# A sketched-attention and gated-convolution kernel: bf16 matmuls in 64-column tiles, one store per output block, and a new order of steps

## The chip, the cores and the metric

The kernel runs on one core of a Trainium2 chip. The metric is the device time of one execution in microseconds (us). The *span*, from the first to the last event of the core, is some 1.7 us shorter. All times within a trace are counted from the start of the span.

A run is called slow when it is more than 1.5% above the fastest of its kernel.

## The reference, cut to what matters

```python
def phi(x):                                   # S1, S2: 8 x 32
    a = einsum('rd,bhsd->bhsr', S1, x);  b = einsum('rd,bhsd->bhsr', S2, x)
    return einsum('bhsi,bhsj->bhsij', a, b).reshape(..., 64)
q_p, k_p = phi(q), phi(k)                     # q, k, v: (4, 4, 1088, 32) float32
kv  = einsum('bhsf,bhsd->bhfd', k_p, v);   z = sum(k_p, axis=2)
x   = einsum('bhsf,bhfd->bhsd', q_p, kv) / (einsum('bhsf,bhf->bhs', q_p, z)[..., None] + 1e-06)
x   = x.transpose(0, 2, 1, 3).reshape(4, 1088, 128)
gate_pre = causal convolution of x along s with conv_w (5 taps, per channel)
out = (sigmoid(gate_pre) * (x @ w_val)) @ w_out          # (4, 1088, 128)
```

## The kernel before: the parts that matter here

The names that the profile shows, in the order of the data: `kT`, `qT` are transposes of k and q in 32x32 blocks on VectorE; `abk`, `abq` their projections on TensorE (f32, 64-column tiles); `ab_sb` the copy of `abk`, `phik` the products a*b of it; `kv` the sums over the sequence (f32, 32-column tiles); `phiq` the normalised features of q (bf16); `pt` their transposes on TensorE and `phiT` the copies of those. For each batch `wg` (kv with the convolution's taps) and `kw` (kv with w_val) are the weights of the gate `g_ps` and the value `v_ps`. `gate` is the sigmoid, `gv` the product, `o_ps` the output, `o_sb` its copy that is stored. There are twelve pieces of k and of q (four batches by three) and 13 output groups. The first 128-column matmuls, `warm_ps`, work on zeros to keep TensorE busy.

The order of all steps is one list, and the program gives every engine its instructions in that order. In the words of that list, `kab.5` is the `abk` of piece 5, `wm.0.512` a zero matmul of 512 columns.

```python
    SP.dma_start(out=s_raw[:r], in_=S1)
    SCA.dma_start(out=s_raw[r:], in_=S2)
    load_units(k, k_sb, 0, 0, 1)              # on SyncE (SP)
    load_units(k, k_sb, 0, 1, U)
...
                PE.transpose(                 # q_pt: full 128-column tiles
                    pt[:, g, t], phq[i, x][:, 2 * t + g].rearrange("p h i j -> p (h i j)"), identity
                )
...
            PE.matmul(                        # g_val
                v_ps[:, :n], lhsT=kw[b][:, g, :], rhs=flat[:, g, c0 : c0 + n],
                start=(g == 0), stop=(g == 1),
            )
...
            if one_store(i):                  # g_st: the last four groups
                (SCA if i == len(GROUPS) - 1 else SP).dma_start(out=rows, in_=src)
            else:                             # the first nine: four stores, or six
                for m in range(nm):
                    SP.dma_start(out=rows[:, m], in_=src[J * m : J * (m + 1)])
...
    ORDER = """
    s2 wm.0.512 wm.1.512 f3.3 f3.1 pad f1 kT.0 f3.0 mz kab.0 kcp.0 cw wm.2.512 kz.0 wm.3.256 kT.1
    ...
```

The whole kernel:

## Time and profile before

| | before |
|---|---|
| median of three runs (lowest, highest), us | 63.55 (62.36, 63.57) |
| span of the profiled run, us | 59.9 |
| first `abk`, first `abq` start | 5.19, 9.74 |
| first `g_ps` starts, last `gv` ends | 18.35, 54.54 |
| last computing ends, last SyncE issue ends | 55.28, 57.08 |

The table cuts the run into three parts: a *start* to the first `abq`, a *middle* to the end of the last `gv` (44.8 us), and a *tail* to the end of the span (5.3 us).

### The profile page before, as it was taken

How to read it: one execution, taken by the hardware profiler on the slowest of the kernel's cores; microseconds unless marked ns; L12 is line 12 of the kernel's file. 1: busy time of each engine (PE TensorE's matmuls, PEld its weight loads, DVE VectorE, ACT ScalarE, POOL GpSimd, SP SyncE). 2: the span in 40 equal slices, each digit the busy share in tenths (PEclk: the TensorE clock that was granted, in tenths of full speed). 3: DMA queues.
4: the chain of work that ended last, by engine and by line, in shares of the span. 5: the costliest groups of instructions: out<-in, count | busy, mean ns of one | idle time of the engine just before them, and what ended most of it. 6: DMA issues, size and time to landing. Idle time of an engine off the chain costs nothing.

```text
span 59.9 us, 2553 instructions
## 1 busy us (share of the span) xinstructions
PE 50.7 (85%) x1003; PEld 36.2 (60%) x1003; DVE 44.3 (74%) x127; ACT 34.7 (58%) x96; POOL 31.8 (53%) x81
## 2 busy tenths in 40 slices
PE   1998988999799899987999999779999999994000
PEld 0224556887586697866985868458876676661000
DVE  2289949998699997994998899357794999836000
ACT  0830241638976688999328759315988776945000
POOL 5653589899995386998829959800420040000000
PEclk9999999999999999999999999999999999999985
DMA  0299997998894587720767421324042223421380
GB/s 0 53 341 370 375 280 236 285 241 238 252 341 141 171 236 211 250 69 5 236 188 189 144 66 44 104 70 109 3 111 69 55 77 99 107 67 34 73 305 5
DMA packets 9254, 9.35 MB, mean 156 GB/s; under 512 B 1941, under 2 KB 9242, under 8 KB 9242
## 3 DMA queue, kind: packets, MB, share of 16 engines
q1 hardware_dynamic: 9072, 9.05, 50.7%
q8 instruction: 8, 0.13, 0.9%
q10 hardware_dynamic: 170, 0.13, 0.7%
q14 instruction: 4, 0.03, 0.3%
HBM read 6.95 MB, written 2.23 MB: 153 GB/s over the span
## 4 chain that ended last, share of the span: by engine, by line
PE 60%; DVE 15%; ACT 8%; issue 4%; POOL 4%; DVEq 0%; ACTq 0%
PE kv L72 12%; PE g_ps L72 11%; PE abq L72 10%; PE abk L72 7%; PE v_ps L72 5%; PE pt L72 5%; PE warm_ps L72 4%; DVE gv L72 4%; DVE wg L72 3%; POOL phik L72 3%; PE wg_ps L72 2%; PE o_ps L72 2%; DVE o_sb L72 2%; ACT wg L72 2%; DVE kT L72 1%
## 5 line engine op out<-in xcount | busy, mean ns | idle before, releaser
L72 POOL TENSOR_TENSOR phik<-ab_sb 128x256 f32<-128x256 f32 x33 | 19.9, 629 | 0.3 <-ACT ab_sb L72 0.3
L72 DVE TENSOR_TENSOR phiq<-an,abq 128x768 bf16<-128x768 f32 (+2 forms) x13 | 11.2, 881 | 0.1
L72 PE MATMUL g_ps<-phiT,wg 128*64 128x384 bf16 (+3 forms) x130 | 11.0, 307 | 0.1
L72 ACT COPY phiT<-pt 128x768 bf16<-128x768 bf16 (+2 forms) x13 | 9.7, 753 | 1.9 <-PE pt L72 1.7
L72 PEld LDWEIGHTS <-wg 128*64 128x64 bf16 x130 | 7.2, 109 | 2.0 <-issue 0.4
L72 ACT ACTIVATE gate<-g_ps 128x384 bf16<-128x384 f32 (+3 forms) x13 | 5.8, 457 | 4.3 <-PE g_ps L72 4.1
L72 DVE TENSOR_TENSOR gv<-gate,v_ps 128x256 bf16<-128x256 bf16 (+3 forms) x14 | 6.1, 456 | 2.8 <-PE v_ps L72 1.5
L72 PE MATMUL abq<-rhsq,qT 128*64 128x96 f32 x144 | 7.7, 251 | 0.2 <-ACT rhsq L72 0.2
L72 PE MATMUL kv<-phik,v_sb 128*32 128x64 f32 x288 | 6.7, 223 | 1.1 <-DVE zm L72 0.6
L72 DVE STREAM_TRANSPOSE kT<-k_sb 128x384 f32<-128x384 f32 x12 | 7.3, 627 | 0.0
L72 PE MATMUL abk<-S,kT 128*64 128x64 f32 x144 | 6.8, 234 | 0.2 <-DVE kT L72 0.2
L72 DVE STREAM_TRANSPOSE qT<-q_sb 128x384 f32<-128x384 f32 x12 | 6.6, 555 | 0.3 <-DMA q_sb<-in_q_dram 0.3
L72 PEld LDWEIGHTS abq<-rhsq,qT 128*64 128x64 f32 x144 | 6.3, 136 | 0.8 <-POOL phiT L72 0.3
L72 PEld LDWEIGHTS abk<-S,kT 128*64 128x64 f32 x144 | 5.6, 144 | 1.7 <-DVE kT L72 1.1
L72 POOL TENSOR_TENSOR prod<-ac 128x96 f32<-128x96 f32 x6 | 2.3, 389 | 7.8 <-ACT ac L72 4.8
L72 PE MATMUL pt<-identity,phiq 128*128 128x128 bf16 x72 | 6.2, 219 | 0.2 <-ACT phiT L72 0.2
L72 ACT COPY ab_sb<-abk 128x192 f32<-128x192 f32 x11 | 3.5, 319 | 4.8 <-PE abk L72 4.7
L72 PE MATMUL warm_ps<-zeros 128*128 128x512 bf16 (+1 forms) x11 | 5.0, 529 | 1.3 <-DVE hm L72 1.3
L72 PEld LDWEIGHTS kv<-phik,v_sb 128*32 128x32 f32 x288 | 4.8, 109 | 2.1 <-DVE zm L72 0.9
L72 PE MATMUL v_ps<-phiT,kw 128*128 128x384 bf16 (+3 forms) x26 | 5.8, 308 | 0.2 <-issue 0.2
L72 PEld LDWEIGHTS <-phiq 128*128 128x128 bf16 x72 | 4.8, 98 | 1.3 <-DVE rden L72 0.4
L72 ACT COPY o_sb<-o_ps 128x384 f32<-128x384 f32 (+3 forms) x13 | 4.8, 399 | 0.9 <-PE o_ps L72 0.8
(77 smaller groups left out, 65.9 us busy)
## 6 DMA issues: line engine op xcount, KB each, us to landing
v_sb<-in_v_dram SPq DMA_DIRECT2D x15, 144.0 KB, 3.7
q_sb<-in_q_dram SPq DMA_DIRECT2D x8, 192.0 KB, 3.5
k_sb<-in_k_dram SPq DMA_DIRECT2D x7, 192.0 KB, 4.2
out_dram<-o_sb SPq DMA_DIRECT2D x24, 48.0 KB, 1.6
q_sb<-in_q_dram SPq DMA_DIRECT2D x4, 160.0 KB, 3.5
k_sb<-in_k_dram SPq DMA_DIRECT2D x3, 160.0 KB, 4.6
k_sb<-in_k_dram SPq DMA_DIRECT2D x1, 384.0 KB, 3.3
out_dram<-o_sb SPq DMA_DIRECT2D x12, 32.0 KB, 1.6
```

The costliest lines, as they stand in the source:

```text
L72: return lambda *a, **k: tc.keep_in_program_order(call(*a, **k))
```

## The change

It has four parts, meant to take work and waits from TensorE, VectorE and SyncE's queue: all bf16 matmuls go in 64-column tiles, so that TensorE changes its tiling mode less often (34 times in the program where it was 53); each output block is stored at once, with its columns in (j,m) order, a row order that makes the store one regular transfer; the first piece of k is issued by ScalarE and the second half of S by SyncE; and the list of steps is a new one. The diff, cut to its core:

```diff
-    SCA.dma_start(out=s_raw[r:], in_=S2)
-    load_units(k, k_sb, 0, 0, 1)
-    load_units(k, k_sb, 0, 1, U)
+    load_units(SCA, k, k_sb, 0, 0, 1)
+    SP.dma_start(out=s_raw[r:], in_=S2)
+    load_units(SP, k, k_sb, 0, 1, U)
...  (the memsets of wg go ahead of the wait for S; the two S products become one;
...   kT of batch 0 is written straight; v of batch 0 is loaded in quarters as the others)
-                PE.transpose(
-                    pt[:, g, t], phq[i, x][:, 2 * t + g].rearrange("p h i j -> p (h i j)"), identity
-                )
+                for y in range(2):
+                    PE.transpose(
+                        pt[R2 * y : R2 * (y + 1), g, t],
+                        phq[i, x][:, 2 * t + g, y].rearrange("p i j -> p (i j)"), identity,
+                    )
...  (v_ps, kw_ps and o_ps are halved in the same way)
+    def by_rows(i, x):
+        lo = 0
+        for _, nc_, nm in blocks(i):
+            hi = lo + nc_ * nm * J
+            yield lo, hi, x[:, lo:hi].rearrange("p (m c j) -> p c j m", m=nm, c=nc_)
+            lo = hi
...  (sigmoid and gv read PSUM through by_rows and write in (j,m) order)
-            if one_store(i):
-                (SCA if i == len(GROUPS) - 1 else SP).dma_start(out=rows, in_=src)
-            else:
-                for m in range(nm):
-                    SP.dma_start(out=rows[:, m], in_=src[J * m : J * (m + 1)])
+            (SCA if i == len(GROUPS) - 1 else SP).dma_start(out=dst, in_=src)
...
-    s2 wm.0.512 wm.1.512 f3.3 f3.1 pad f1 kT.0 f3.0 mz kab.0 kcp.0 cw wm.2.512 kz.0 wm.3.256 kT.1
+    kT.0 s2 wm.0.256 pad kab.0 kcp.0 cw wm.1.512 kT.1 kT.2 kz.0 kab.1 mz kcp.1 kab.2 wm.2.256 kz.1
...  (the whole list differs)
```

More of the change, by code (lines that the diff above doesn't have):

```diff
@@ L106, in load, with load_units @@
         )
-    def load_units(src, dst, b, u0, u1):
+    def load_units(eng, src, dst, b, u0, u1):
         lo, n = NCK * u0 * D, NCK * (u1 - u0) * D
-        SP.dma_start(
+        eng.dma_start(
             out=dst[b].rearrange("p (m x) -> p m x", m=M4)[:, :, lo : lo + n],
@@ L114, in load_units @@
                 tensor=src.tensor, offset=src[b].offset + lo, ap=[[NT * D, P], [TM * D, M4], [1, n]]
-            ),
-        )
-    def v_head(b, h):
-        SP.dma_start(
-            out=v_sb[b][:, h].rearrange("p T d -> p (T d)"),
-            in_=bass.AP(
-                tensor=v.tensor, offset=v[b, h].offset, ap=[[NT * D, J], [TM * D, M4], [1, TM * D]]
             ),
@@ L139, in load_v @@
         for x in (0, 2, 1, 3):
-            (v_head if b == 0 else v_quarter)(b, x)
+            v_quarter(b, x)
     def load_k(b):
@@ L193, with fill_3 @@
         DVE.memset(hm[h * D : (h + 1) * D, h : h + 1], 1.0)
+    wg = [ctile([P, 2, KT, 2 * D], BF16, f"wg{b}") for b in range(B)]
+    def fill_3(eng, b):
+        for x in range(2):
+            eng.memset(wg[b][R2 * x : R2 * (x + 1), :, :, D * (1 - x) : D * (2 - x)], 0.0)
+    fill_3(DVE, 0)
+    fill_3(DVE, 1)
     m2 = ctile([P, 2], F32, "m2")
@@ L204 @@
     keep_warm(2)
-    for x in range(2):
-        DVE.tensor_mul(
-            S3[:, x].rearrange("p (h r) -> p h r", h=H),
-            st_ps[:, x].unsqueeze(1).to_broadcast([P, H, r]),
-            hm.unsqueeze(2).to_broadcast([P, H, r]),
-        )
+    DVE.tensor_mul(
+        S3.rearrange("p x (h r) -> p x h r", h=H),
+        st_ps.unsqueeze(2).to_broadcast([P, 2, H, r]),
+        hm.unsqueeze(1).unsqueeze(3).to_broadcast([P, 2, H, r]),
+    )
     mz4 = ctile([P, H, H], F32, "mz4")
@@ L224 @@
     dcw = ctile([P, KT, D], F32, "dcw")
-    wg = [ctile([P, 2, KT, 2 * D], BF16, f"wg{b}") for b in range(B)]
     POOL.memset(w_val_sb, 0.0)
@@ L263, in fill_2 @@
             POOL.memset(phiT[b][:, :, 0].rearrange("p g (T j) -> p g T j", j=J)[:, :, :, 0:1], 0.0)
-    def fill_3(eng, b):
-        for x in range(2):
-            eng.memset(wg[b][R2 * x : R2 * (x + 1), :, :, D * (1 - x) : D * (2 - x)], 0.0)
     def pad_k():
@@ L305, in k_T @@
         DVE.transpose(
-            out=kT[b][:, u * W : (u + 1) * W].rearrange(
-                "p (t m j) -> p t m j" if b else "p (t j m) -> p t m j", t=NCK, m=M4
-            ),
+            out=kT[b][:, u * W : (u + 1) * W].rearrange("p (t m j) -> p t m j", t=NCK, m=M4),
             in_=k_sb[b].rearrange("p (m u t d) -> p u t m d", m=M4, u=U, t=NCK)[:, u],
@@ L429, in kw_mm @@
         kwp[b] = ps_k.tile([P, 2, P], F32, tag="k", name="kw_ps")
-        PE.matmul(kwp[b], lhsT=kvt[b].rearrange("p x f -> p (x f)"), rhs=w_val_sb, start=True, stop=True)
+        for x in range(2):
+            PE.matmul(
+                kwp[b][R2 * x : R2 * (x + 1)], lhsT=kvt[b][:, x], rhs=w_val_sb, start=True, stop=True
+            )
     def kw_ev(eng, b):
@@ L502, in q_pt @@
             for g in range(2):
-                PE.transpose(
-                    pt[:, g, t], phq[i, x][:, 2 * t + g].rearrange("p h i j -> p (h i j)"), identity
-                )
+                for y in range(2):
+                    PE.transpose(
+                        pt[R2 * y : R2 * (y + 1), g, t],
+                        phq[i, x][:, 2 * t + g, y].rearrange("p i j -> p (i j)"), identity,
+                    )
         pts[i, x] = pt
@@ L524 @@
     GROUPS = [(b, T0, min(TU, NT - T0)) for b in range(B - 1) for T0 in range(0, NT, TU)]
-    ONE = 9
     GROUPS += [(B - 1, 0, 12), (B - 1, 28, 6), (B - 1, 12, 8), (B - 1, 20, 8)]
@@ L553, in g_val @@
         for g in range(2):
-            PE.matmul(
-                v_ps[:, :n], lhsT=kw[b][:, g, :], rhs=flat[:, g, c0 : c0 + n],
-                start=(g == 0), stop=(g == 1),
-            )
-        vps[i] = v_ps
-    def g_sig(i):
-        _, n, _ = columns(i)
-        gate = work.tile([P, W], BF16, tag="gate", name="gate")
-        SCA.activation(out=gate[:, :n], in_=gps[i][:, :n], func=ACT.Sigmoid)
-        gts[i] = gate
+            for y in range(2):
+                ys = slice(P // 2 * y, P // 2 * (y + 1))
+                PE.matmul(
+                    v_ps[ys, :n], lhsT=kw[b][:, g, ys], rhs=flat[:, g, c0 : c0 + n],
+                    start=(g == 0), stop=(g == 1), skip_group_check=True,
+                )
+        vps[i] = v_ps
     def blocks(i):
@@ L570, in blocks, with rows, g_sig @@
         return [(T0, *whole[n])] if n in whole else [(T0, 2, M4), (T0 + 2 * M4, 1, n - 2 * M4)]
-    def one_store(i):
-        return i >= ONE
+    def by_rows(i, x):
[4 more added lines that the diff above has]
+            lo = hi
+    def rows(x, lo, hi, like):
+        return x[:, lo:hi].rearrange("p (c j m) -> p c j m", j=J, m=like.shape[3])
+    def g_sig(i):
+        gate = work.tile([P, W], BF16, tag="gate", name="gate")
+        for lo, hi, x in by_rows(i, gps[i]):
+            SCA.activation(out=rows(gate, lo, hi, x), in_=x, func=ACT.Sigmoid)
+        gts[i] = gate
     def g_gv(eng, i):
@@ L582, in g_gv @@
         gv = work.tile([P, W], BF16, tag="gv", name="gv")
-        lo = 0
-        for _, nc_, nm in blocks(i):
-            hi = lo + nc_ * nm * J
-            order = "p c j m" if one_store(i) else "p c m j"
-            def cols(x):
-                return x[:, lo:hi].rearrange(f"p (m c j) -> {order}", m=nm, c=nc_)
-            eng.tensor_mul(
-                gv[:, lo:hi].rearrange(f"p ({order[2:]}) -> {order}", c=nc_, m=nm), cols(gts[i]), cols(val)
-            )
-            lo = hi
+        for lo, hi, x in by_rows(i, val):
+            eng.tensor_mul(rows(gv, lo, hi, x), rows(gts[i], lo, hi, x), x)
         gvs[i] = gv
@@ L603, in g_out @@
             for c in range(nc_):
-                PE.matmul(
-                    o_ps[: nm * J, c0 + c, :], lhsT=gvs[i][:, lo : lo + nm * J], rhs=w_out_sb,
-                    start=True, stop=True,
-                )
+                for y in range(0, nm * J, P // 2):
+                    PE.matmul(
+                        o_ps[y : y + P // 2, c0 + c, :], lhsT=gvs[i][:, lo + y : lo + y + P // 2],
+                        rhs=w_out_sb, start=True, stop=True,
+                    )
                 lo += nm * J
@@ L625, in g_st @@
             src = osb[i][: J * nm, c0 : c0 + nc_].rearrange("p c e -> p (c e)")
-            rows = o_d[:, T0 : T0 + nm * nc_].rearrange("j (m c) e -> j m (c e)", m=nm)
-            if one_store(i):
-                (SCA if i == len(GROUPS) - 1 else SP).dma_start(out=rows, in_=src)
-            else:
-                for m in range(nm):
-                    SP.dma_start(out=rows[:, m], in_=src[J * m : J * (m + 1)])
+            dst = o_d[:, T0 : T0 + nm * nc_].rearrange("j (m c) e -> j m (c e)", m=nm)
+            (SCA if i == len(GROUPS) - 1 else SP).dma_start(out=dst, in_=src)
             c0 += nc_
@@ L648 @@
     ORDER = """
-    s2 wm.0.512 wm.1.512 f3.3 f3.1 pad f1 kT.0 f3.0 mz kab.0 kcp.0 cw wm.2.512 kz.0 wm.3.256 kT.1
-    sr.0 kT.2 kab.1 kab.2 kp.0.0 kcp.1 srA.1 kz.1 kcp.2 kz.2 wm.4.256 qT.1 qT.0 zm.0 c.0 wm.5.256
-    kpV.2.2 kpV.0.2 qab.0 qab.1 kT.3 kT.5 qcp.0 kp.1.1 kp.1.2 kab.3 f2 qcp.1 kkv.1.2 kpV.2.1 kT.4
-    kp.2.0 kp.1.0 qpr.0 kp.0.1 kkv.2.0 kcp.3 kkv.2.2 kab.5 kkv.1.0 qden.0 qprV.1 qrc.0 kp.3.1 ldq.3
-    kkv.1.1 kkv.2.1 qden.1 kkv.0.2 kkv.0.0 ldk.2 kcp.5 qanV.0 w kp.5.0 qrc.1 qphi.0 kkv.0.1 kvx.0
@@ L654 @@
-    kab.4 qpt.0 kp.3.0 qT.2 qanV.1 kp.5.1 qphi.1 qab.2 kcp.4 qev.0 qcp.2 kp.4.0 qT.3 kvtA.0 ldq.4
-    kp.3.2 qprV.2 kz.3 wgm.0 kz.4 kkv.5.0 kkv.3.1 kz.5 kkv.4.0 ldq.5 zm.1 wge.0.0 wge.0.1 kkv.5.1
-    kkv.3.0 qden.2 c.1 kwm.0 kwe.0 kT.6 qrc.2 qpt.1 kp.4.1 qev.1 qab.3 halo.0 ldk.3 qcp.3 kab.6
-    kp.5.2 kp.4.2 gmm.0 qpr.3 val.0 kcp.6 sig.0 qanV.2 qphi.2 qT.5 qden.3 qpt.2 ldq.8 ldq.6 qrc.3
-    kT.7 qan.3 qphi.3 kkv.3.2 qT.4 kkv.4.1 kkv.4.2 kT.8 kkv.5.2 gvP.0 kvx.1 qev.2 kp.6.2 ldv.2 kab.7
-    qab.5 qcp.5 kcpV.7 qab.4 kT.9 qpr.5 o.0 qpt.3 qcp.4 srA.2 oev.0 wgm.1 gmm.1 kvtA.1 wge.1.0 gmm.2
@@ L660 @@
-    qprV.4 wge.1.1 qden.4 qden.5 qev.3 qrc.4 kp.7.2 qan.4 qrc.5 kab.8 kz.6 ldq.7 f3.2 kcp.8 qanV.5
-    qphi.4 kp.7.0 kp.7.1 kp.6.0 sig.1 haloA.1 kp.8.1 qpt.4 qT.6 val.2 kwm.1 val.1 kz.7 kp.8.0 st.0
-    qphi.5 kkv.8.1 qT.8 kkv.6.2 kz.8 kkv.8.0 kkv.6.0 kkv.7.2 qev.4 kp.8.2 kwe.1 kkv.7.0 gvP.1 sig.2
-    zm.2 ldq.11 kT.10 cV.2 qT.7 kab.9 ldq.9 kcp.9 qab.6 qab.7 gv.2 qcpV.6 kp.6.1 qprV.6 qden.6 gmm.3
-    kab.10 qrc.6 kkv.6.1 srA.3 ldq.10 sig.3 kcp.10 kkv.7.1 kkv.8.2 kvx.2 qpt.5 val.3 wgm.2 qcpV.7
@@ L665 @@
-    kT.11 o.2 qan.6 qphi.6 qev.5 kp.9.1 oev.2 qpr.7 qden.7 wgeV.2.0 gv.3 qab.8 kp.10.2 qcpV.8 qprV.8
-    wge.2.1 kab.11 kp.10.0 qden.8 gmm.4 kcp.11 sig.4 kp.10.1 gmm.5 kp.9.0 ldv.3 sig.5 kz.9 qrc.7
-    qan.7 qrc.8 qan.8 o.3 kp.9.2 val.4 o.1 st.2 qpt.6 qT.10 oev.3 kz.10 kp.11.0 kp.11.2 qphi.7
-    kkv.10.1 kkv.9.0 oev.1 kz.11 qev.6 kkv.9.2 qphi.8 kp.11.1 kkv.11.2 st.3 kkv.10.2 kkv.10.0
-    kkv.11.0 zm.3 kkv.9.1 c.3 gv.4 qT.9 kkv.11.1 val.5 kvtP.2 qpt.7 qab.10 qab.9 o.4 gv.5 qev.7
-    qcp.9 kvxV.3 kwm.2 qcpV.10 qpr.10 haloV.2 qpt.8 oev.4 o.5 qprV.9 qev.8 oev.5 kwe.2 qden.10
@@ L671 @@
-    qden.9 qrc.10 qT.11 gmm.6 gmm.8 sig.6 sig.8 gmm.7 qan.10 qrc.9 wgm.3 sig.7 kvtA.3 val.7 val.6
-    qphi.10 qan.9 qphi.9 qpt.9 wge.3.1 gv.7 qev.9 o.7 qab.11 val.8 st.1 qcp.11 wgeV.3.0 oevV.7 gv.6
-    st.4 qpr.11 qpt.10 halo.3 kwm.3 qev.10 o.6 gv.8 qden.11 o.8 st.5 gmm.10 oevV.6 qrc.11 qanV.11
-    gmm.9 st.7 qphi.11.0 kwe.3 oev.8 sig.10 sig.9 st.6 val.10 qpt.11.0 val.9 qev.11.0 qphi.11.1
-    gv.10 qpt.11.1 qev.11.1 st.8 gv.9 o.10 gmm.11 val.11 oev.10 gmm.12 sig.11 val.12 gv.11 st.10 o.9
-    sig.12 gv.12 o.11 oev.9 st.9 o.12 oev.12 oevV.11 st.11 st.12
+    kT.0 s2 wm.0.256 pad kab.0 kcp.0 cw wm.1.512 kT.1 kT.2 kz.0 kab.1 mz kcp.1 kab.2 wm.2.256 kz.1
@@ new lines @@
+    kcp.2 srA.0 qT.0 kp.0.2 qT.1 kz.2 wm.3.256 sr.1 zm.0 kpV.2.1 kpV.0.0 c.0 wm.4.256 kpV.1.2 kT.3
+    qab.1 ldq.3 qab.0 kp.0.1 kp.1.1 kp.1.0 qcp.1 kT.5 kab.3 qcp.0 kT.4 kcp.3 kp.2.2 f1 qpr.0 kab.5
+    qden.0 kcp.5 qprV.1 kp.2.0 kab.4 qrc.0 kkv.0.2 kp.3.1 kkv.2.0 kcp.4 kkv.1.2 kkv.1.0 kp.3.2
+    qden.1 qanV.0 qrc.1 qphi.0 qan.1 kkv.2.2 kkv.1.1 kkv.2.1 kkv.0.1 kkv.0.0 qT.2 kvxV.0 qpt.0
+    kvtA.0 qev.0 qab.2 kp.5.1 kz.3 wgm.0 kz.4 wge.0.0 kkv.5.1 f2 qphi.1 w kz.5 qcpV.2 kkv.3.1 kp.3.0
+    kp.4.0 halo.0 qprV.2 qden.2 zm.1 kkv.3.2 qpt.1 qT.3 wge.0.1 c.1 kp.5.0 qrc.2 kkv.4.0 qanV.2
@@ new lines @@
+    kkv.3.0 ldk.2 kwm.0 kp.5.2 qphi.2 qev.1 kT.6 kp.4.1 qab.3 ldq.4 kwe.0 gmm.0 qT.4 val.0 qcp.3
+    kab.6 qpr.3 kp.4.2 ldq.5 qpt.2 kkv.4.2 ldk.3 qden.3 qrc.3 qan.3 sig.0 kT.7 kkv.5.2 gvP.0 kcp.6
+    qT.5 ldq.6 kkv.4.1 kkv.5.0 ldv.2 kab.7 qev.2 qphi.3 kp.6.2 qab.4 ldq.7 o.0 kvx.1 kcp.7 kT.8
+    qcpV.4 kT.9 kp.7.1 kp.6.0 qprV.4 wgm.1 oev.0 kp.7.2 kz.6 kvtP.1 qden.4 qrc.4 qT.6 srA.2 wge.1.0
+    st.0 kp.6.1 qanV.4 qT.7 val.2 qab.5 wge.1.1 kab.8 gmm.2 kp.7.0 kcp.8 kwm.1 qpt.3 qcp.5 sig.2
+    qphi.4 gmm.1 gv.2 kz.7 kkv.6.0 kkv.7.2 kp.8.1 qev.3 qpr.5 qden.5 kp.8.2 qrc.5 kwe.1 kz.8 kp.8.0
@@ new lines @@
+    zm.2 qanV.5 sig.1 val.1 srV.3 kab.9 gvP.1 qphi.5 o.2 kT.10 qpt.4 oev.2 kkv.8.0 f3P.2 halo.1
+    ldq.8 ldq.9 qT.8 ldv.3 kkv.6.1 kcp.9 kkv.7.0 f3P.3 kkv.7.1 c.2 kkv.8.1 kkv.8.2 kkv.6.2 o.1 qev.4
+    ldq.10 st.2 kT.11 qab.6 kab.10 gmm.3 qcp.6 qprV.6 qden.6 qrc.6 qanV.6 oev.1 kvx.2 kcp.10 qphi.6
+    val.3 qab.8 qpt.5 sig.3 kp.9.2 gv.3 qcp.8 kz.9 wgm.2 ldq.11 wgeV.2.0 qab.7 kp.9.1 qev.5 kp.10.1
+    qcp.7 o.3 gmm.4 oev.3 wge.2.1 qT.11 sig.4 qT.10 kab.11 gmm.5 qpt.6 qpr.8 kp.9.0 kcp.11 qden.8
@@ new lines @@
+    kp.10.0 val.4 qpr.7 sig.5 kp.10.2 qden.7 qrc.7 qrc.8 qanV.7 kkv.10.2 kvtA.2 kp.11.1 kz.10
+    kkv.10.0 kp.11.0 qphi.7 kkv.9.0 kkv.9.1 kz.11 qan.8 kkv.9.2 kkv.11.1 kkv.10.1 gvP.4 kpV.11.2
+    kkv.11.0 qev.6 st.1 zm.3 kkv.11.2 c.3 qT.9 qphi.8 val.5 halo.2 st.3 qpt.7 o.4 qev.7 qab.9 qab.10
+    qcp.9 oevV.4 gv.5 qpt.8 qcp.10 qpr.9 kvxV.3 o.5 kwm.2 qev.8 oev.5 qpr.10 gmm.6 qden.9 gmm.8
+    kwe.2 qden.10 sig.6 gmm.7 wgm.3 qrc.9 qrc.10 sig.8 qanV.10 sig.7 qan.9 kvtP.3 val.7 qphi.9
+    qphi.10 val.6 wge.3.1 wge.3.0 st.4 qpt.9 val.8 gv.7 o.7 qev.9 gv.6 qab.11 o.6 gv.8 oevV.7 oevV.6
@@ L677 @@
+    qcp.11 qpr.11 qden.11 qpt.10 qrc.11 o.8 qanV.11 qev.10 kwm.3 oev.8 gmm.10 halo.3 gmm.9 kwe.3
+    sig.10 qphi.11.0 st.5 sig.9 val.10 qphi.11.1 qpt.11.0 st.7 val.9 gv.10 qev.11.0 st.6 o.10 oev.10
+    qpt.11.1 st.8 gv.9 qevV.11.1 gmm.11 sig.11 st.10 val.11 gv.11 gmm.12 sig.12 val.12 o.11 o.9
+    oev.11 gv.12 o.12 oev.12 st.11 oevV.9 st.9 st.12
     """
```

## The prediction

*Drain* is the name for the surplus of some 95 ns between the starts of matmuls at a change of tiling mode. The traces show the surplus (150 ns where 56 to 60 were due), not what TensorE does in it.

> **What bounds the kernel now.** I read the page first: busy shares and the chain of work that ended last.
>
> ```profile
> PE 50.7 (85%) x1003; PEld 36.2 (60%) x1003; DVE 44.3 (74%) x127; ACT 34.7 (58%) x96; POOL 31.8 (53%) x81
> ...
> PE 60%; DVE 15%; ACT 8%; issue 4%; POOL 4%; DVEq 0%; ACTq 0%
> ```
>
> TensorE has 60% of the chain, in many small pieces (kv, g_ps, abq, abk, v_ps, pt). VectorE is second, at 74% busy. So what matters most is what TensorE pays per stage, then the two ends of the run, where other things bind. I next read TensorE's timeline where it changes from one kind of matmul to another. Columns: start, length, engine, line, operation, tile form, count.
>
> ```profile
> 13.01 0.57 PE L72 MATMUL abk<-S,kT 128*64 128x64 f32 x12
> 13.51 0.51 PE L72 MATMUL pt<-identity,phiq 128*128 128x128 bf16 x6
> 13.95 0.79 PE L72 MATMUL abq<-rhsq,qT 128*64 128x96 f32 x12
> ...
> 18.35 1.00 PE L72 MATMUL g_ps<-phiT,wg 128*64 128x384 bf16 x10
> 19.29 0.34 PE L72 MATMUL v_ps<-phiT,kw 128*128 128x384 bf16 x1
> ```
>
> One transpose lasts 0.22 us in its record, so the six start every (0.51-0.22)/5, about 56 ns, and the last starts at 13.80. The first abq starts at 13.95, 150 ns later. The surplus is about 95 ns. Backwards likewise: the last abk starts at 13.01+0.57-0.22 = 13.36, the first transpose 150 ns later, where two of abk's matmuls stand some 60 ns apart. From g_ps to v_ps it is about 260 ns where 384 columns take 160. **Each change between a 64-column and a 128-column tile costs about 95 ns**, whatever the types. This kernel has its f32 work and the gate in 64-column tiles, but the bf16 transposes, v_ps, kw and o_ps in full ones.
>
> Then the beginning, on VectorE:
>
> ```profile
> 2.35 0.21 DVE L72 COPY s_nat<-s_raw 16x128 f32<-16x128 f32 x1 [0.70 <-DMA s_raw<-in_S_dram]
> 3.00 0.29 DVE L72 TENSOR_TENSOR S<-st_ps,hm 128x32 f32<-128x32 f32 x2 [0.44 <-PE st_ps L72]
> 3.27 0.98 DVE L72 MEMSET wg<- 64x160 uint32 x4
> 4.28 0.85 DVE L72 STREAM_TRANSPOSE kT<-k_sb 128x384 f32<-128x384 f32 x1
> ...
> 10.86 0.55 DVE L72 STREAM_TRANSPOSE kT<-k_sb 128x384 f32<-128x384 f32 x1
> ```
>
> Four memsets stand before the first k transpose, on the chain, while VectorE had idled 0.70 us before. The first transposes write in (j,m) order and take 0.85 us; later ones write straight and take 0.55.
>
> Then the end: the queue of SyncE, ScalarE's store and the last copies.
>
> ```profile
> 49.98 7.10 SPq L72 DMA_DIRECT2D out_dram<-o_sb  x12
> ...
> 55.32 0.62 ACTq L72 DMA_DIRECT2D out_dram<-o_sb  x1
> ...
> 53.94 0.59 DVE L72 TENSOR_TENSOR gv<-gate,v_ps 128x256 bf16<-128x256 bf16 x1 [0.40 <-ACT gate L72]
> 54.45 0.41 DVE L72 COPY o_sb<-o_ps 128x256 f32<-128x256 f32 x1
> ```
>
> The last block that SyncE stores is ready at 54.86, but SyncE issues its last store only at 57.08, after a backlog of quarter stores. Nothing computes after 55.28; the span ends at 59.9.
>
> [...] The trace has 98 ns for a full bf16 load and 109 for a 64-column one, but they lie beside matmuls; whether they show in the spacing I judge below. [...] for strided PSUM reads no clean case exists in it. [...] a SyncE issue takes 0.4 to 0.6 us.
>
> **The change, part by part.**
>
> *Tile mode.* I counted mode changes in the order of the matmuls of both programs: 53 before, 34 after, so 19 fewer; all but one lie after the start, where the 128-column tiles disappear altogether. 19 x 95 ns = 1.8 us of TensorE. What the halves cost: a transpose becomes two of 64 columns in two tiles that run side by side. g_ps does this already: ten matmuls of 384 columns in 1.00 us, that is five pairs of about 160 ns, the time of one. abk pairs, of 64 columns with two f32 weight loads, stand about 60 ns apart, so a load pair fits in 60. I take 56 to 64 ns per transpose pair, against 56 now: 72 x 0 to 8 ns, at most 0.6 us lost. v_ps, o_ps and kw stream as long as before. Net on TensorE 1.2 to 1.8 us; with TensorE on the chain over most of 9.7 to 46 us, but handing over to VectorE and GpSimd at 22-26, 33-38 and 46-49 us, I count two thirds: **-1.1 us**.
>
> *Start.* The memsets move into VectorE's wait: 1.0 us off. The first k transposes fall from 0.85 to 0.55: three times 0.3. The first k piece leaves ScalarE at 0.81 instead of SyncE at 1.27. Against it, the second half of S goes out second on SyncE, about 0.3 us later, and so does everything from s_nat on. The first transpose should start near 3.5 instead of 4.28 and abk near 4.3 instead of 5.19. The first abq (9.74 now) then comes some 1 to 1.5 us earlier. Not all can survive, since v of the first batch lands only near 9.5 to 10 us: **-0.9 us**.
>
> *Stores.* Four SyncE issues of about 0.42 us become one of about 0.58. The backlog goes. Now it takes 57.08-54.53 = 2.55 us from the end of the last gv to the end of the last issue. After: matmuls 0.3, eviction 0.37, ScalarE's issue 0.62, with gaps 1.4 us; SyncE's last store (eviction 0.56, issue 0.6) fits beside it. **-1.1 us.**
>
> *Order of (j,m) rows.* The late gv, which already reorders, takes 0.81 us for 384 columns and 0.59 for 256:
>
> ```profile
> L72 DVE TENSOR_TENSOR gv<-gate,v_ps x4: 206/460/553, 29.3 to 38.7; 128x384 bf16<-128x384 bf16 x2, 128x256 bf16<-128x256 bf16 x1, 128x64 bf16<-128x64 bf16 x1
> ...
> L72 DVE TENSOR_TENSOR gv<-gate,v_ps x1: 808/808/808, 51.5 to 51.5; 128x384 bf16<-128x384 bf16 x1
> ```
>
> It reads both the gate (SBUF) and v_ps (PSUM) with a stride. After, only PSUM is read with a stride, by the sigmoid and by gv. If SBUF was the cost, every gv takes 0.55 and the tail gains 0.2; if PSUM is as dear, seven earlier gv lose 0.2 each on VectorE and thirteen sigmoids some 0.2 on ScalarE. I hold the first likelier (60%). The sigmoid of the 320-column groups is split, three times 0.15 us on ScalarE, which has room.
>
> *New order.* Going down both VectorE lists with the durations above, VectorE loses some 2 us (fewer and cheaper kT, memsets, copies of ac and wg), GpSimd gains about 2. That unloads the second bound and loads one with 47% idle: **-0.3 us**, uncertain in sign.
>
> Sum: -1.1-0.9-1.1-0.3 = -3.4 us; I take off 0.2 for the strided reads: -3.2 of 59.9, a span of about 56.7. 63.55 x 56.7/59.9 = **60.2 us**.
>
> **Rivals.** (1) *TensorE isn't the bound in the middle*: the 19 drains vanish into waits on VectorE and GpSimd. For it: VectorE is nearly always busy from 9 to 38 us, and phik on GpSimd alone takes 19.9 us. Against: TensorE's 60% of the chain. Then only the two ends count: -1.8 us, about 61.6. (2) *64-column weights are slower*: [...] say 80 ns a pair: 72 x 24 ns = 1.7 us, which eats the drains saved. Against: abk's pairs at 60. About 61.4. (3) *PSUM stride dear and GpSimd late*: phik and gv on GpSimd push kv back; with the first two gains kept about 61.5. (4) *All add up, and the earlier start pulls everything with it*: -4.5 us, about 58.8.
>
> **Range and chances.** Runs of before lie between 62.36 and 63.57, so 1.2 us of spread is there without any change. From rivals 1 to 4: 58.2 to 62.0. Under 2% is 1.3 us; the two ends alone give more, so faster 0.87, same 0.11, slower 0.02.
>
> **What would show it.** Right: pt, v_ps and o_ps in 64-column form with the transposes' pairs 56 to 64 ns apart; no 95 ns surplus between them and abq, abk or g_ps; the first abk near 4.3 and abq near 8.5; SyncE's last issue within 1.5 us of the last gv; gv of 384 columns at 0.55. Wrong: transpose pairs at 80 ns; sigmoids at 0.7; a middle stretch as long as before with longer waits of TensorE for phik or den; a start that waits for v. The prediction fails if the span stays over 58.5.

## More of the kernel before

Within the middle, the stretch from the first `g_ps` to the last `gv` turns out to be the best yardstick of this case. Here is the busy time in it for the kernel before, from the view of windows (window, its length, busy us and instructions of each engine, TensorE clock, DMA share and rate):

```profile
18.35:54.54 36.19, 34.22 (x670) 25.45 (x666) 29.71 (x81) 25.59 (x69) 17.51 (x35) 1.00 0.40 113
```

TensorE (the first figure after the length) is busy 95% of this stretch.

(The table further down takes the stretch from the unrounded times, so it can differ by 0.01 us from the views.)

## The result

The changed kernel took 59.65 us (median of four runs, 58.91 to 60.37), the kernel before 62.95 us in the same rounds (four runs, 62.03 to 63.57). The ratio of the fast runs is 0.9475, with a 95% interval of 0.9365 to 0.9585: faster. A ratio is the mean time of one kernel's fast runs over that of the other's fast runs of the same rounds, so not quite the ratio of the medians quoted. Two of the four runs of the changed kernel were slow (spans 58.5 and 58.6 against 57.2). The profile is of a fast one.

| us | before | after | change | predicted |
|---|---|---|---|---|
| start: first `abq` starts | 9.74 | 10.45 | +0.7 | -0.9 |
| middle: first `abq` to end of last `gv` | 44.8 | 42.4 | -2.4 | -1.1 (tiles) -0.3 (order) |
| tail: end of last `gv` to end of span | 5.3 | 4.4 | -0.9 | -1.1 (stores) |
| span | 59.9 | 57.2 | -2.6 | -3.2, with +0.2 for strided reads |

**The whole.** Busy shares and the chain of what ended last, from the page of the changed kernel:

```profile
PE 48.1 (84%) x1135; PEld 37.0 (65%) x1135; DVE 42.3 (74%) x120; ACT 35.0 (61%) x99; POOL 34.6 (60%) x87
...
PE 80%; ACT 5%; DMA 4%; issue 2%; DVE 1%; SPq 1%; DVEq 0%
```

TensorE is 2.6 us less busy in spite of 132 more instructions, and its share of the chain has risen from 60% to 80%: VectorE and GpSimd, which had 15% and 4%, are all but gone from it.

**The middle.** TensorE's timeline of the changed kernel where kinds of matmul meet (start, length, form, count):

```profile
19.86 0.98 PE L72 MATMUL g_ps<-phiT,wg 128*64 128x384 bf16 x10
20.67 0.49 PE L72 MATMUL v_ps<-phiT,kw 128*64 128x384 bf16 x4
21.00 0.52 PE L72 MATMUL abk<-S,kT 128*64 128x64 f32 x12
21.34 0.50 PE L72 MATMUL pt<-identity,phiq 128*64 128x128 bf16 x12
21.78 0.65 PE L72 MATMUL kv<-phik,v_sb 128*32 128x64 f32 x32
```

With 0.22 us for one, the twelve half transposes, six pairs whose two halves start 3 ns apart, take a step of (0.50-0.22)/5 = 56 ns a pair, as one full transpose did before (56 ns). The last `abk` starts at about 21.00+0.52-0.22 = 21.30 and the first transpose some 50 ns after it (55 from the unrounded starts), where there were 150. But from the last transpose (21.62) to `kv`, in 32-column tiles, it is still 150 to 160 ns. So the surplus is there for a change of mode, and gone where the mode is now the same.

The same stretch as above, in the view of windows of the changed kernel:

```profile
19.86:52.84 32.98, 32.08 (x801) 26.16 (x796) 28.04 (x75) 26.30 (x75) 20.66 (x40) 1.00 0.41 125
```

It is 3.2 us shorter. VectorE has 1.7 us less to do in it and GpSimd (the fifth figure) 3.2 more. The middle as a whole wins less, since the first `g_ps` comes 9.4 us after the first `abq` instead of 8.6. That is not more work: TensorE has twelve `abk` matmuls less on this leg than before (and twelve more in the stretch), but it is idle for 1.55 us of it, where it was for 0.31. Two of its waits in the changed kernel:

```profile
12.43 0.57 PE L72 MATMUL abk<-S,kT 128*64 128x64 f32 x12 [0.42 <-ACT ab_sb L72]
...
18.87 0.43 PE L72 MATMUL kv<-phik,v_sb 128*32 128x64 f32 x16 [0.40 <-ACT rhsq L72]
```

The first kind comes twice: the new order sets three pieces of k one after the other, and the second and third each wait 0.42 us until ScalarE has copied the piece before out of its single PSUM buffer.

**The start.** The timelines of VectorE and TensorE of the changed kernel:

```profile
3.57 0.21 DVE L72 COPY s_nat<-s_raw 16x128 f32<-16x128 f32 x1 [0.84 <-DMA s_raw<-in_S_dram]
4.36 0.57 DVE L72 STREAM_TRANSPOSE kT<-k_sb 128x384 f32<-128x384 f32 x1
...
5.51 0.91 PE L72 MATMUL abk<-S,kT 128*64 128x64 f32 x12
...
7.35 1.55 PE L72 MATMUL abk<-S,kT 128*64 128x64 f32 x24
...
10.45 1.21 PE L72 MATMUL abq<-rhsq,qT 128*64 128x96 f32 x24
```

and TensorE's of the kernel before:

```profile
5.19 0.91 PE L72 MATMUL abk<-S,kT 128*64 128x64 f32 x12 [0.19 <-DVE kT L72]
...
7.16 0.92 PE L72 MATMUL abk<-S,kT 128*64 128x64 f32 x24
...
9.74 1.21 PE L72 MATMUL abq<-rhsq,qT 128*64 128x96 f32 x24 [0.18 <-ACT rhsq L72]
```

The transposes are cheaper as planned (0.57 where 0.85 was), but `s_nat` starts at 3.57 instead of 2.35, for S came later. Near its beginning the chain of the changed kernel has that transfer (start, length):

```profile
1.29 2.19 DMA s_raw<-in_S_dram
```

And a second thing: the second group of `abk` takes 1.55 us for 24 where it took 0.92. TensorE's clock record in the trace begins, at full speed, at 9.05 us in the changed kernel and at 6.66 us before. The page and the windows count the time without a record as full; that the clock is slower until then is inference from the matmuls: pairs of `abk` start 107 ns apart before these moments and 58 ns apart after them, in both traces. "Full clock" below means the start of this record.

**The tail.** ScalarE's, SyncE's and VectorE's timelines of the changed kernel at the end:

```profile
47.33 6.75 SPq L72 DMA_DIRECT2D out_dram<-o_sb  x7
...
53.64 0.63 ACTq L72 DMA_DIRECT2D out_dram<-o_sb  x1
...
50.23 0.56 DVE L72 TENSOR_TENSOR gv<-gate,v_ps 128x384 bf16<-128x384 bf16 x1 [0.25 <-PE v_ps L72]
...
52.42 0.42 DVE L72 TENSOR_TENSOR gv<-gate,v_ps 128x256 bf16<-128x256 bf16 x1 [0.34 <-ACT gate L72]
```

SyncE's last issue ends at 54.08 and ScalarE's at 54.27, 1.4 us after the last `gv`, where it was 2.5. The late `gv` of 384 columns takes 0.56 us, not 0.81, though v_ps is still read with a stride.

### The profile page after: what moved, and what is told of

It reads as the page before.

```text
span 57.2 us, 2783 instructions
## 1 busy us (share of the span) xinstructions
PE 48.1 (84%) x1135; PEld 37.0 (65%) x1135; DVE 42.3 (74%) x120; ACT 35.0 (61%) x99; POOL 34.6 (60%) x87
## 3 DMA queue, kind: packets, MB, share of 16 engines
HBM read 6.95 MB, written 2.23 MB: 160 GB/s over the span
## 4 chain that ended last, share of the span: by engine, by line
PE 80%; ACT 5%; DMA 4%; issue 2%; DVE 1%; SPq 1%; DVEq 0%
PE g_ps L72 16%; PE kv L72 14%; PE abq L72 11%; PE abk L72 11%; PE pt L72 8%; PE v_ps L72 7%; PE o_ps L72 4%; DMA s_raw<-in_S_dram 4%; PE warm_ps L72 4%; PE wg_ps L72 3%; ACT phiT L72 1%; ACT o_sb L72 1%; ACT ab_sb L72 1%; DVE zm L72 1%; ACT rhsq L72 1%
## 5 line engine op out<-in xcount | busy, mean ns | idle before, releaser
L72 POOL TENSOR_TENSOR phik<-ab_sb 128x256 f32<-128x256 f32 x32 | 19.3, 628 | 0.7 <-ACT ab_sb L72 0.6
L72 ACT COPY phiT<-pt 128x768 bf16<-128x768 bf16 (+1 forms) x12 | 9.4, 781 | 0.8 <-PE pt L72 0.8
L72 POOL TENSOR_TENSOR prod<-ac 128x96 f32<-128x96 f32 x8 | 3.1, 390 | 7.6 <-ACT ac L72 7.3
L72 PEld LDWEIGHTS abk<-S,kT 128*64 128x64 f32 x144 | 6.3, 159 | 1.9 <-ACT ab_sb L72 1.1
L72 DVE STREAM_TRANSPOSE kT<-k_sb 128x384 f32<-128x384 f32 x12 | 6.4, 551 | 0.9 <-DMA k_sb<-in_k_dram 0.9
L72 PE MATMUL pt<-identity,phiq 128*64 128x128 bf16 x144 | 6.5, 221 | 0.0
L72 DVE TENSOR_TENSOR gv<-gate,v_ps 128x256 bf16<-128x256 bf16 (+3 forms) x13 | 4.9, 405 | 1.6 <-ACT gate L72 1.0
L72 PE MATMUL v_ps<-phiT,kw 128*64 128x384 bf16 (+3 forms) x52 | 5.8, 309 | 0.0
L72 PEld LDWEIGHTS <-phiq 128*64 128x64 bf16 x144 | 5.2, 110 | 0.5
L72 ACT COPY ac<-abq 128x192 f32<-128x192 f32 x10 | 3.2, 320 | 3.0 <-PE abq L72 2.2
```

The lines of the kernel that those rows point to most:

```text
L72: return lambda *a, **k: tc.keep_in_program_order(call(*a, **k))
```

## The experiments

Twelve runs were made, of eleven new kernels and once more of the changed one. The three questions: why the middle won more than predicted, what the stores are worth, and what the start lost.

The main result comes first, since six of the runs bear on it. "Changes of mode" counts the places where neighbouring matmuls have different tiling modes (the tile form of the timeline, as `128*64`; `96*32` counts as `128*32`, since the starts of the two are only 35 or 36 ns apart): in the program, and in brackets in the trace within the stretch from the first `g_ps` to the last `gv`. The last column has the spans of the fast runs.

| kernel | tiles | order | stores | changes of mode | stretch, us | fast spans, us |
|---|---|---|---|---|---|---|
| before | wide | old | quarters | 53 (32) | 36.18 | 59.5 to 60.6 |
| b_tiles | narrow | old | quarters | 36 (18) | 36.05 | 61.0, 61.7 |
| b_stores | wide | old | whole | 53 (32) | 35.87 | 58.6 |
| a_oldorder | narrow | old | whole | 36 (18) | 35.21 | 60.7 to 61.4 |
| n_oldorder | narrow | old | whole | 36 (18) | 35.21 | 59.2 |
| b_order | wide | new | quarters | 71 (51) | 36.47 | 63.4 to 63.6 |
| a_wide | wide | new | whole | 71 (51) | 36.23 | 60.4, 60.8 |
| w_ptwide | `pt` alone wide | new | whole | 54 (35) | 34.57 | 58.2 to 58.4 |
| a_quarters | narrow | new | quarters | 34 (16) | 34.83 | 60.3 |
| after | narrow | new | whole | 34 (16) | 32.98 | 57.0 to 57.2 |

Where the clock was full by 9.21 us, the stretch repeats: it is 32.98 us to 10 ns in all five traces of the changed kernel and of the three variants that keep its tiles, order and stores. Four rows have only a trace with a later clock: a_oldorder, n_oldorder, b_order and a_wide.

### Tiles alone on the kernel before: b_tiles

```diff
 before
-                PE.transpose(pt[:, g, t], phq[i, x][:, 2 * t + g]...
+                for y in range(2):
+                    PE.transpose(pt[R2 * y : R2 * (y + 1), g, t], phq[i, x][:, 2 * t + g, y]...
 (and kw_ps, v_ps, o_ps likewise)
```

> The kernel before with one part of the change alone: bf16 transposes, v_ps, kw and o_ps in 64-column tiles; order, loads and stores as before. Mode changes in program order fall from 53 to 36, 17 x 95 ns = 1.6 us of TensorE. Theory (TensorE bounds the middle, drains lie on it): span 58.5 to 58.9 against 59.9, ratio 0.977 to 0.985. Rival 1 (drains vanish into waits on VectorE and GpSimd): ratio 0.995 to 1.0. Rival 2 (64-column weights slower): transpose pairs near 80 ns apart, ratio 1.0 or more.

Measured: 63.69 us median (62.67 to 64.50, four runs, two slow) against 62.04 for before. The gain expected from the tiles did not come: with 14 changes of mode fewer, the stretch became only 0.13 us shorter. From the page of b_tiles, the chain, and the window:

```profile
PE 38%; DVE 25%; ACT 9%; DMA 6%; POOL 4%; issue 4%; SPq 2%; DVEq 0%; ACTq 0%
```

```profile
18.29:54.34 36.05, 33.64 (x791) 26.91 (x786) 30.16 (x81) 25.28 (x69) 17.44 (x34) 1.00 0.42 118
```

TensorE's busy time fell by 0.6 us, the length did not: the other engines took over the chain. What makes the run longer than before lies in the tail: last `gv` at 54.34, as before, but the end at 61.7. Most issues on SyncE take 0.3 to 0.6 us (77 of 87 before, 51 of 57 in the changed kernel). Nine of SyncE's 87 issues took over 0.8 us in this trace (five of 87 before, up to 1.48), and the quarter stores queue behind them. Why more issues stalled, no run shows.

### The new order alone on the kernel before: b_order

```diff
 before
-    s2 wm.0.512 wm.1.512 f3.3 f3.1 pad f1 kT.0 f3.0 mz kab.0 ...
+    f3.0 f3.1 kT.0 s2 wm.0.256 pad kab.0 kcp.0 cw wm.1.512 ...   (all of the new list)
```

> The kernel before with the new order alone (the two first memsets of wg put at the head of the order). In program order it has 71 mode changes against 53, 18 more, 1.7 us of TensorE. If the order was drawn up for 64-column tiles and drains count: slower than before, ratio 1.01 to 1.03. If the order is what made the middle shorter and drains don't count: faster, ratio 0.96 to 0.98.

Measured: 65.34 us median, ratio 1.0554 (1.0470 to 1.0638): slower by its interval, though the record's verdict is "unclear". Its profile fell on a slow run whose clock was full only from 18.76 us, so its start says little. Its stretch does: 36.47 us with 51 changes of mode, against 36.18 with 32. In the wide kernel the new order buys nothing, since it sets 19 more changes of mode in the stretch, by estimate 1.8 us at 95 ns each.

### Wide tiles in the changed kernel: a_wide

```diff
 after
-                for y in range(2):
-                    PE.transpose(pt[R2 * y : R2 * (y + 1), g, t], ...
+                PE.transpose(pt[:, g, t], phq[i, x][:, 2 * t + g]...
 (and kw_ps, v_ps, o_ps likewise)
```

> The changed kernel with the bf16 matmuls and transposes put back into 128-column tiles; order, stores and loads stay. In the new order this makes 71 mode changes of 34, 37 more, 37 x 95 ns = 3.5 us of TensorE, which the chain of the changed kernel shows on TensorE for 80% of the span. Theory (in the new order the drains lie on the bound): span 60.0 to 60.9 against 57.2, ratio to before 1.00 to 1.02. Rival (as in the old order, where 17 fewer drains ended the compute only 0.2 us earlier, they vanish into waits): span 57.2 to 58.0, ratio 0.95 to 0.96.

Measured: 63.17 us median, ratio 1.001 (0.9915 to 1.0104). The fast spans of 60.4 and 60.8 are 3.2 to 3.6 us above those of the changed kernel, as the theory had it. The profile is of a slow run (clock full at 14.1 us), but its stretch is clean:

```profile
21.56:57.78 36.22, 35.48 (x682) 24.77 (x678) 28.11 (x75) 26.80 (x74) 20.80 (x40) 1.00 0.37 109
```

Here TensorE is busy 98% of the time (97% in the changed kernel). So in the new order the narrow tiles win 36.23-32.98 = 3.25 us of 35 fewer changes: 93 ns for each, all of it in the length.

### The transposes alone wide: w_ptwide

```diff
 a_warm (below)
-                for y in range(2):
-                    PE.transpose(pt[R2 * y : R2 * (y + 1), g, t], ...
+                PE.transpose(pt[:, g, t], phq[i, x][:, 2 * t + g]...
```

> This is a_warm with the transposes alone back in full 128-column tiles, all else narrow: 54 mode changes in program order against 34, 72 fewer TensorE instructions. It takes the cost of a mode change in the new order by itself, from a start that is clean. Theory: 20 more changes of 95 ns are 1.9 us of TensorE, which has 80% of the chain, so the span grows by 1.4 to 2.0 us, to 57.6 to 58.4; ratio .955 to .97. Rival, that a_wide lost its 3.2 us mostly through its late full clock: the span grows by less than 0.8 us, to at most 57.0, ratio under .945.

Measured: 59.99 us median (59.92 to 60.09, all four fast), ratio 0.9677 (0.9608 to 0.9745), spans of 58.2 to 58.4 against 56.1 to 56.5 of a_warm. The theory holds and its rival, that a_wide lost mostly by its late clock, falls. TensorE's timeline and the window:

```profile
20.56 0.53 PE L72 MATMUL abk<-S,kT 128*64 128x64 f32 x12
21.02 0.51 PE L72 MATMUL pt<-identity,phiq 128*128 128x128 bf16 x6
21.45 0.65 PE L72 MATMUL kv<-phik,v_sb 128*32 128x64 f32 x32
```

```profile
19.42:54.00 34.58, 33.82 (x741) 26.24 (x736) 28.58 (x76) 26.72 (x75) 20.73 (x40) 1.00 0.44 131
```

The last `abk` starts at 20.56+0.53-0.22 = 20.87 and the transpose 150 ns later. The six full transposes themselves take the time of the twelve halves. With 51, 35 and 16 changes of mode the stretch is 36.23, 34.57 and 32.98 us: 104 and 84 ns per change, on both sides of the 95 ns read from the trace before any run. The 84 compares two traces with an early clock; the 104 rests on the late one of a_wide.

### The old order in the changed kernel: a_oldorder and n_oldorder

```diff
 after (a_oldorder), a_s2act below (n_oldorder)
-    kT.0 s2 wm.0.256 pad kab.0 kcp.0 cw wm.1.512 ...
+    s2 wm.0.512 wm.1.512 f3.3 pad f1 kT.0 mz kab.0 ...     (all of the old list)
```

> The changed kernel with the order of before (without the two memsets now done at the start). Tiles, one store each, rows and loads stay; 36 mode changes. Theory (tile mode and order only pay together): the compute ends near 54.5 to 55, the tail is 3.6 us, span 58.3 to 59.2, ratio 0.975 to 0.985. Rival (tiles and stores do it all, the order nothing): span near 57.2, ratio 0.945 to 0.955.

> This is a_s2act (64-column tiles, one store per block, S2 back on ScalarE) with the order of steps of the kernel before, so that the start is the old one too, unlike a_oldorder, where S2 came late and TensorE got its full clock only at 15.8 us. 36 mode changes in program order against 34. Theory, that the new order is itself worth 1 to 2 us once the tiles are narrow (b_tiles: with the old order the narrow tiles won only 0.2 us of computing): full clock before 8 us, abk near 4.4, the span 57.5 to 58.5 against 56.3 to 56.6 of a_s2act, ratio to the kernel before .955 to .975. Rival, that tiles and stores do it all and the order only shuffles work: span 56.0 to 56.6, ratio .935 to .945.

Measured: a_oldorder 62.96 us median, ratio 1.0104 (1.0024 to 1.0184), where 58.3 to 59.2 us of span were expected and 61.3 came; n_oldorder 62.63 us median (60.91 to 63.05), three of four runs slow, so no ratio, and one fast span of 59.2. Both profiles have a spoilt start: the clock was full only from 15.82 and 16.18 us. That n_oldorder was meant to have a clean one is a miss. Its TensorE timeline shows what a late clock costs (24 `abq` in 2.19 us; in the lines above they take 1.21):

```profile
10.82 2.19 PE L72 MATMUL abq<-rhsq,qT 128*64 128x96 f32 x24
```

The stretch after it has the full clock, and both traces give the same 35.21 us:

```profile
21.35:56.56 35.21, 33.44 (x784) 26.63 (x784) 28.82 (x81) 25.45 (x72) 17.88 (x34) 1.00 0.38 118
```

TensorE's share of n_oldorder's chain is 61%, against 80% in the changed kernel. So with narrow tiles the old order is 2.23 us longer than the new one in the stretch; taking off the 0.8 us by which the changed kernel comes later from the first `abq` to the first `g_ps`, the order is worth about 1.4 us. That is an estimate, since neither profile has a clean start. The late clock seems to have helped the old order's stretch: its first leg, to the second `g_ps` group, takes 4.7 us in both these traces, and 5.3 in b_tiles, where the clock was early and TensorE waits 0.31 us for VectorE's `qT`. So 35.21 may be up to 0.6 us too short; no run settles it. The rival, that tiles and stores do it all, falls: they leave the stretch at 35.21.

### The stores: b_stores and a_quarters

```diff
 b_stores: before
-            if one_store(i): ...  else: for m in range(nm): SP.dma_start(out=rows[:, m], ...)
+            (SCA if i == len(GROUPS) - 1 else SP).dma_start(out=dst, in_=src)
 (with the sigmoid and gv in (j,m) order for all groups)
 a_quarters: after
+            if i >= 9: (one store)
+            else:
+                for m in range(nm):
+                    SP.dma_start(out=dst[:, m], in_=src[J * m : J * (m + 1)])
 (and these nine groups keep the column order of before)
```

> The kernel before with the sigmoid and gv writing in (j,m) rows and one store for each block, nothing else. Theory: SyncE's backlog at the end goes; from the end of the last gv to the span's end 4.3 us instead of 5.3, gv of the late groups 0.55 instead of 0.81; span 58.6 to 58.9, ratio 0.975 to 0.985. Rival: the stores were hidden and the tail is the writes' own latency: ratio 0.995 to 1.0.

> The changed kernel with quarter stores for the first nine blocks, as before; all else stays. Theory (SyncE's backlog sets the end): SyncE's last issue ends 1.5 to 2.5 us after the last compute instead of 0.65, span 58.0 to 58.9, ratio 0.96 to 0.975. Rival (tail hidden): span 57.2, ratio 0.947.

Measured: b_stores 62.0 us median (60.29 to 62.40), one run fast and three slow, so its time is unclear against 62.04. Its profile, of the fast run, has a tail of 4.36 us from the last `gv`, where before had 5.32 and the changed kernel 4.39: the step of the stores holds in size. a_quarters took 63.87 us median (62.13 to 66.88), spans from 60.3 (the fast one) up, where 58.9 at most was expected. The tail is one reason: 7.0 us in its profile, which fell on a slow run (61.3), with the last issue at 58.67. The other was not foreseen. The chain of a_quarters in the middle, and TensorE's timeline after it:

```profile
33.80 3.39 DMA q_sb<-in_q_dram
```

```profile
40.68 0.32 PE L72 MATMUL kv<-phik,v_sb 128*32 128x64 f32 x8 [2.17 <-DVE zm L72]
```

A piece of q, issued only at 33.80 after six quarter stores (29.90 to 33.71), holds VectorE until 37.2, and TensorE then runs out of work: it is idle from 38.5 to 40.68. Waits on `zm` take 2.17 us of this stretch against 0.32 in the changed kernel, and these 1.85 us are the whole difference of the stretches (34.83 against 32.98). In the new list the loads of q, k and v share SyncE's queue with 42 stores of the first nine groups instead of 12. So the single stores also keep the loads of the new order in time, which the prediction had not counted.

### The start: a_s2act, a_warm, after_again

```diff
 a_s2act: after
-    load_units(SCA, k, k_sb, 0, 0, 1)
-    SP.dma_start(out=s_raw[r:], in_=S2)
+    SCA.dma_start(out=s_raw[r:], in_=S2)
+    load_units(SP, k, k_sb, 0, 0, 1)
 a_warm: a_s2act, and
-    keep_warm(3)
+    keep_warm(4)
-    kT.0 s2 wm.0.256 pad ...
+    kT.0 s2 wm.0.512 wm.5.512 pad ...
```

> The changed kernel with the loads of S2 and of the first piece of k put back as before (S2 from ScalarE, k from SyncE). In the changed kernel S2, issued 0.5 us after the k piece, has its packets among k's 512 and is waited for until 3.5 us, 1.2 us later than before. Theory (the load move costs the start): s_nat at 2.4 instead of 3.57, the first abk near 4.4 to 4.8 instead of 5.5, the first abq near 9.3 to 9.7 instead of 10.45, and the span 56.2 to 56.6 against 57.2, ratio to before 0.93 to 0.94. Rival (the start is hidden, since v and TensorE's later waits set the pace): span 57.0 to 57.3, ratio 0.947.

> The changed kernel with S2 from ScalarE and k from SyncE again, and three more matmuls on zeros in the first 5 us, as before had. In the traces of before, b_tiles and b_stores the clock record has full speed from 4.6 to 6.7 us, in the changed kernel and a_s2act, with fewer such matmuls, from 9.1 to 9.2, and their 24 abk matmuls take 1.48 us instead of 0.92. Theory: full speed from 4.6 to 6.7 us, 24 abk in 0.9 to 1.0, first abq near 9.2 to 9.5 (0.6 gained, 0.2 to 0.4 lost to the added matmuls), span 55.9 to 56.4, fewer slow runs. Rival (the time of full speed is chance): full speed anywhere from 4.6 to 12 us, span 56.5 to 57.

> The changed kernel once more, unaltered, on the chip of these runs, to have it beside them in the same rounds, and to see whether its start repeats. Theory: fast spans 57.0 to 57.5, ratio .94 to .955, and some runs at about 58.5; S2 landed near 3.5 us, first abk near 5.5, full clock near 8 to 10 us. If the profile falls on a slow run, I expect its full clock later than 10 us or a stall of an issue of SyncE over 0.8 us.

Measured: a_s2act 58.30 us median, ratio 0.9412 (0.9332 to 0.9491), fast spans of 56.4 to 56.6. `s_nat` moved from 3.57 to 2.76, the first `abk` from 5.51 to 4.70 and the first `abq` from 10.45 to 9.73, and the end by the same 0.7 us. So this part of the change was a loss, and taking it back is faster than the changed kernel. But `s_nat` was expected at 2.4, where it was before. VectorE's timeline of a_s2act shows what is left:

```profile
1.75 0.98 DVE L72 MEMSET wg<- 64x160 uint32 x4
2.76 0.21 DVE L72 COPY s_nat<-s_raw 16x128 f32<-16x128 f32 x1
```

The four memsets that the change moved ahead of `s_nat` take 0.98 us, and VectorE's wait there had only been 0.70 (see the prediction's lines). So they hold `s_nat` back by 0.4 us; in the changed kernel, where VectorE still waits 0.84 us for S after them, the late S hides this.

a_warm, with more zero matmuls at the start (12 instead of 10, and one twice as long): 58.10 us median (57.94 to 58.28, all four fast), ratio 0.9334 (0.9296 to 0.9372). The clock was full at 6.12 us instead of 9.21, and the second group of `abk` took 0.92 again. TensorE's timeline of a_warm:

```profile
1.27 1.89 PE L72 MATMUL warm_ps<-zeros 128*128 128x512 bf16 x4 [1.27 <-DVE hm L72]
...
6.86 0.92 PE L72 MATMUL abk<-S,kT 128*64 128x64 f32 x24
```

The first `abk` itself waits 0.6 us longer for the added zeros, but `abq` starts at 9.33.

after_again, the changed kernel unaltered beside the last three: 59.53 us median, ratio 0.9484 (0.9376 to 0.9591), two fast spans of 57.0 and 57.1 and two slow ones of 58.4 and 58.6; first `abk` at 5.45, clock full at 8.35. The result repeats.

### A version meant to beat both: n_best

```diff
 a_warm
-        pool, tag = (ps_g, "g") if i < U else (ps_k, "k")
+        pool, tag = (ps_g, "g") if i < U or i == 5 else (ps_k, "k")
-            SCA.copy(out=val[:, :n], in_=vps[i][:, :n])
+            for lo, hi, x in by_rows(i, vps[i]):
+                SCA.copy(out=rows(val, lo, hi, x), in_=x)
```

> A version that should beat both: a_warm with two changes. The sixth piece of k in the order of piece numbers (5) takes its PSUM tile from the pool with three buffers, as the first three do, since TensorE waited twice 0.42 us at 10.5 to 13 us for ScalarE to clear the single buffer of the other pool; and the copies of v_ps that ScalarE makes for GpSimd are written in (j,m) order, so that GpSimd's gv reads SBUF straight: 1.13 to about 0.92 us for 384 columns, with ScalarE's copy unchanged or up to 0.2 us longer. Theory: span 55.5 to 56.1 against 56.1 to 56.5 of a_warm, ratio .92 to .93. Rival, that later waits take up what the start gains: span 56.1 to 56.5, ratio .93 to .937.

Measured: 58.21 us median (57.08 to 58.65), two runs fast (spans 55.3 and 56.1) and two slow (56.8, 56.9), ratio of the fast ones 0.9411 (0.9298 to 0.9525). Its best run is the fastest of the study, but its median does not beat that of a_warm. Both edits do what they should: GpSimd's `gv` falls to 0.92 us and the two waits of `abk` are gone. What they are worth is less clear. The stretch stays at 32.98 us, so the cheaper `gv` buys nothing there. The first `g_ps` comes at 17.92 instead of 19.00, but the clock too was full earlier, at 4.53 us. From groups by tile, GpSimd's `gv` (count, shortest/mean/longest in ns, when) in the changed kernel and in n_best:

```profile
L72 POOL TENSOR_TENSOR gv<-gate,val x3: 1117/1131/1137, 21.9 to 38.6; 128x384 bf16<-128x384 bf16 x3
```

```profile
L72 POOL TENSOR_TENSOR gv<-gate,val x3: 913/919/929, 19.9 to 36.7; 128x384 bf16<-128x384 bf16 x3
```

### What the late clock has to do with it

Of the fourteen traces, ten have the full clock by 9.21 us, and four (b_order, a_wide, a_oldorder, n_oldorder) only from 14.1 to 18.76. Three of these four are of slow runs. The one slow profile with an early clock (8.3 us) is a_quarters. This would fit a slow state that is mostly a late full clock, but all four runs of a_oldorder are fast by the rule, though its trace has one. The pairs of a slow and a fast trace of one kernel that would show it were not taken, so this stays open. The clock listed with each run cannot decide it, since it counts the time without a record as full.

## Why the prediction was right or wrong

The time, the range and the direction were right: 60.2 us predicted, 59.65 measured. That the sum came out so close is in part luck: two terms missed in opposite directions, the start by 1.6 us and the middle by 1.0. The starting point was chance too: the predicted saving of 3.2 us of span was set on 63.55 us, the median of three runs, while the profiled run took 61.57; the profiles differ by 2.6.

**Start, predicted -0.9, measured +0.7: the sign was wrong.** The prediction named the risk, "the second half of S goes out second on SyncE, about 0.3 us later", and gave it too little: `s_nat` came 1.2 us later. And "the memsets move into VectorE's wait: 1.0 us off" put 0.98 us of memsets into a wait of 0.70, which the prediction's own lines show; a_s2act has the 0.4 us that this costs at `s_nat`. The trace of the changed kernel shows S on the path from 1.29 to 3.48 us, its packets (1.77 to 2.91 us) among the 512 of the piece of k that ScalarE had issued just before (1.93 to 3.11); a_s2act shows that undoing this alone brings 0.7 us. A further part was not in the prediction at all: the new list has fewer zero matmuls early on, and the clock was full 2.4 us later. That the first causes the second is what a_warm suggests, with more zeros and an earlier clock, but the clock also varies between kernels with the same list (full at 6.12 us in a_warm, at 4.53 in n_best). a_s2act still started `abq` at 9.73, no earlier than before; 9.33 and 8.62 came only in a_warm and n_best, where the clock was full at 6.12 and 4.53. The "near 8.5" of the prediction was all but reached in n_best, but not in this kernel.

**Tiles and order, predicted -1.4 together, measured -2.4 in the middle: right in the cost of a change, wrong in size and in how it was split.** The 95 ns are confirmed (84 to 104 per change), and rival 2, slow weights in narrow tiles, is refuted: pairs at 56 ns, not the 80 assumed. (The prediction's (0.51-0.22)/5 gives 58 ns, not 56; the single starts in the trace before are 67 and then 55 or 56 ns apart, so its 56 and its 95 stand.) The step that failed is "I count two thirds". In these runs the share depended on what else was on the chain. In the old order, with TensorE at 60% of the chain, 14 fewer changes won 0.13 us with quarter stores (b_tiles) and 0.66 at most with whole ones (35.87 to 35.21, the latter with the late clock), of 1.3; there rival 1 describes what happened. In the new order all of it shows (93 ns per change, a_wide). And the term "-0.3" for the order was mis-sized because it was priced by itself: with wide tiles it costs 0.3 to 0.4 us of the stretch, with narrow tiles and whole stores it wins 2.23 (about 1.4 after its longer way from `abq` to `g_ps`, an estimate). VectorE's loss of some 2 us was right (44.3 to 42.3 us busy), and GpSimd's gain was 2.8 rather than 2 (31.8 to 34.6). What the order does is make TensorE the bound (its share of the chain is 61% in n_oldorder and 80% in the changed kernel); in these runs that was worth something only with the narrow tiles, which give TensorE fewer changes to pay for.

**Stores, predicted -1.1, measured -0.9: right.** The last issue ended 1.4 us after the last `gv`, as worked out. Missing was that in the new order the stores also hold up the loads (a_quarters).

**(j,m) rows: right.** The first guess held, given 60%: here a stride in SBUF was dear (0.81 us), one in PSUM was not (0.55). Every `gv` of 384 columns on VectorE takes 0.55, the sigmoid of 384 takes 0.50 as before, and the 0.2 us set aside for strided reads was not needed. The first part of rival 3 is out. Its second part, GpSimd late, shows as a longer `gv` (1.13 us), but making it shorter moved no end.

## What to carry to other kernels

Count the changes of tiling mode along TensorE's real order: each costs near 95 ns here (84 to 104), and with TensorE as the bound, narrow tiles for all bf16 matmuls were worth 3.25 us of the stretch here even at twice their number of instructions. Ask which engine binds before pricing such a gain: a re-ordering that makes TensorE the bound and a saving on TensorE were worth 0.4 us lost and at most 0.7 us won in the stretch by themselves, and 2.9 us together (35.87 to 32.98). Before moving the first transfers or dropping early work that looks idle, check what the first dependent step waits for, and when TensorE gets its full clock: here `s_nat` came 1.2 us later, and the clock was full 2.4 us later.
